# The second FFN product as Strassen's seven half-size products over pairs of 128-token tiles

## The chip, the cores and the metric

The kernel runs on one core of a Trainium2 chip. Its time is the device time of one execution in microseconds (us). The kernel before was timed three times.

## What is computed

```python
# attention: q, k, v are [4 batches, 8 heads, 768, 64], sort_net [4, 8, 8, 8]
P = sort_net                                   # five rounds: exp, row and column normalisation
k_sorted = einsum('bhij,bhjcd->bhicd', P, k_blocks)      # blocks of 96 rows
v_sorted = einsum('bhij,bhjcd->bhicd', P, v_blocks)
attn = softmax(q_b @ k_sorted_b.T / 8)         # within each of the 8 blocks
x = (attn @ v_sorted_b)  ->  [3072 tokens, 512]
# feed-forward network (FFN): w_in [512, 2048], w_out [2048, 512]
h = maximum(x @ w_in, 0)
out = (h * h) @ w_out                          # float32 [3072, 512]
```

Matrix products take bf16 operands and accumulate in fp32 in PSUM.

## The kernel before

The text counts the batches from 1 to 4 (the code's `b` from 0 to 3). A batch has 768 tokens. Attention of a batch ends in `xT`, the FFN's input, stored transposed: 128 features to a partition, four chunks of features (`kc`), all 3072 tokens along the free side. Both weights stay in SBUF as bf16 (`w_in_bf`, `w_out_bf`).

The FFN works on eight token groups of 384 (`ffn_unit(g)`, two to a batch). For a group it does

- the first product (L1009, tile `hp`): for each of 16 blocks of 128 hidden features (`nt`) four matmuls of 384 columns, each with a weight load of a 128x128 piece of `w_in_bf`. ScalarE takes the sum out of PSUM with a Relu (L1017), VectorE squares it (L1020) into `h2`.
- the second product (L1039, tile `op`): for each of three tiles of 128 tokens 16 matmuls of 512 columns, with pieces of `h2` as the loaded weights and rows of `w_out_bf` streaming. The 512 output columns of 128 tokens fill one PSUM bank. `put` copies them to SBUF (`ob`), and SyncE (SP) starts the DMA to `out`.
- the very last tile of 128 tokens is cut into 384 and 128 columns (`last_tile`, L1067), so that the last copy is small.

Three PSUM banks (pool `psf`, ring `rf`) serve both products; two double banks (`p2`) and one single bank (`p1`) serve attention.

The order of all instructions is fixed when the program is written. `Plan` keeps a list of operations with engine, assumed cost and dependencies. Attention's operations on TensorE (PE) have a due time in chunks of FFN work (table `DUES`: by batch and stage, K, V, N: sorting and loads of k and v; Z: turns of k and q by DMA; S: scores; A: attention times v; X: the turn of the result into `xT`). `Plan.run` plays the operations through and emits each engine's instructions in the resulting order. PE gets attention of batch n+1 between the FFN matmuls of batch n. For batches 2 to 4, X is a DMA transpose that SP issues (L920), only the last one of batch 2 goes through PE (L938); for batch 1 some go through PE and, in the second half, three through the DMA.

Loads of q, k and v for batches 3 and 4 are held back (L1157) until the attention of the batch before is in `xT`.

Of the kernel before, what the change touches and what calls it, by code (L numbers as in the profile page):

```python
# [8 lines left out]
FP32 = mybir.dt.float32  # L9
# [24 lines left out]
    (1, "X"): (40.0, 23.5, 37.0, 53.5),
    (2, "L"): (40.0,),
    (2, "N"): (75.5, 79.0),
    (2, "V"): (60.5, 82.5),
    (2, "Z"): (81.0, 82.5, 94.0, 83.5),
    (2, "S"): (86.0, 86.5, 96.0, 93.5),
    (2, "A"): (86.0, 88.0, 99.0, 94.5),  # L40
    (2, "X"): (97.5, 103.0, 103.0, 102.0),
    (3, "L"): (109.0,),
    (3, "N"): (111.5, 130.0),
    (3, "V"): (112.5, 144.0),
    (3, "Z"): (128.5, 139.0, 153.0, 149.0),
    (3, "S"): (144.0, 153.0, 158.0, 153.5),
    (3, "A"): (145.0, 153.5, 159.5, 154.5),
    (3, "X"): (150.5, 170.0, 236.5, 211.5),
}


# [55 lines left out]

class Plan:
# [6 lines left out]
    SWITCH = 0.1  # L115
    SLACK = {"DMA": 2.5, "WAY": 0.6}
# [19 lines left out]
    def run(self):  # L136
# [4 lines left out]
        while att or ffn or rest:  # L141
# [43 lines left out]
def kernel(  # L185
# [34 lines left out]
    psf = ctx.enter_context(tc.tile_pool(name="psf", bufs=3, space=bass.MemoryType.PSUM))  # L220
# [263 lines left out]
    def p_spread(e, i0):  # L484
        t = tiles["pt_ps", i0] = psf.tile([128, NQ, NH], FP32, tag="pf", name="pt_ps")
# [74 lines left out]
    def s_q(b, hp, p0, p1, due=0, after=None, eng=AD):  # L560
# [4 lines left out]
        def mm(e):  # L565
            qb = qkv[b][0]
            if b == 0:
                t["p"] = psf.tile([128, NA, n], BF16, tag="pf", name="qtp")
# [38 lines left out]
    def s_sort(u, t, due=0, early=False, eng=AD, own=False):  # L607
# [3 lines left out]
        def mm(e):  # L611
            src = qkv[u.b][t]
            if early:
                tp = ((ps1 if own else psf)
                      .tile([128, 512], FP32, tag="p1" if own else "pf", name="tp"))
# [115 lines left out]
    def s_vt(u, due=0, eng=AD, own=True):  # L731
# [95 lines left out]
    def s_turn(u):  # L827
# [10 lines left out]
        def k_blocks(e):  # L838
            nc.vector.tensor_copy(out=u.ksT[:, 0:S].rearrange("p (n x) -> p n x", n=NB),  # L839
                                  in_=kx_r[kx].rearrange("p (x n) -> p n x", n=NB))  # L840
# [4 lines left out]
        u.k_op = plan.add("DVE", 0.87, k_blocks, [k_op] + u.old)  # L845
# [69 lines left out]
    def s_xt(u, due=0, eng=AD, own=True):  # L915
        early = u.b == 0 and u.halves == (1,) and u.hp < HP - 1
# [17 lines left out]
        def mm(e):  # L934
            st["p"] = xtp = ((ps1 if own else psf)
                             .tile([128, u.ni, BLK], BF16, tag="p1" if own else "pf", name="xtp"))
# [21 lines left out]
    def f_piece(n):  # L958
# [3 lines left out]
        def mm(e):  # L962
            if kc == 0:
                tiles["hp", nt] = psf.tile([128, 512], FP32, tag="pf", name="hp")
            nc.tensor.matmul(  # L965
                out=tiles["hp", nt][:, 0:HS], lhsT=w_in_bf[:, kc, 128 * nt:128 * (nt + 1)],
                rhs=xT[:, kc, 0:HS], start=(kc == 0), stop=False)

        old = begun.setdefault((0, nt), [])
        if kc == 0:  # L970
            f_slot[nt], old = rf.take(pin=True)
        pe = plan.add("PE", 0.163, mm, [x_done[0, kc, 0], landed["w_in", 0]] + old)
        rf.use(f_slot[nt], pe)
        begun[0, nt].append(pe)

    def put(key, t, n, dst, pe, g):

        st = {}
        so, old = rob.take()

        def cp(e):
            st["ob"] = ffn.tile([128, d_model], FP32, tag="ob", name="ob", bufs=4)
            copy(e, st["ob"][:, 0:n], t[key][:, 0:n])

        op = plan.add(AD, cost_f(n), cp, [pe] + old)
        last = g == n_tok // HS - 2
        for p in ((slice(0, 32), slice(32, 64), slice(64, 128)) if last else (slice(0, 128),)):
            sp = plan.add("SP", 0.55, lambda e, p=p: nc.sync.dma_start(out=dst[p, :], in_=st["ob"][p, 0:n]), [op])
        rob.use(so, plan.add("WAY", 1.5, lambda e: None, [sp], tail=0.6))
        return op  # L990

    def ffn_unit(g):
        t0 = HS * g
        b, hf = g // 2, g % 2
# [223 lines left out]
```

## Time and profile before

| | |
|---|---|
| device time, three runs | 217.03, 217.30, 217.31 us; median 217.3 us |
| span of the profiled execution, first to last instruction | 215.4 us |
| own time of the profiled execution | the page gives only its span; the median is 1.9 us above it |
| busy: PE, PE weight loads, VectorE (DVE), ScalarE (ACT), GpSimd (POOL) | 210.0, 115.3, 110.3, 122.1, 28.2 us |
| mean granted TensorE clock | 1.000 |
| DMA | 31.92 MB, mean 148 GB/s |

How to read the rows that follow: a group row has line, engine, operation, output and inputs, count, then busy time in us, the mean ns of one, and the idle time before them with what ended it. A matmul's own duration contains the depth of the pipeline; how fast matmuls follow each other is read from the chain, whose pieces have start, length, engine, tile, line and count. In the waits each row is: engine and tile, waiting for what, us in total, times, longest.

### The profile page before, as it was taken

How to read it: one execution, taken by the hardware profiler on the slowest of the kernel's cores; microseconds unless marked ns; L12 is line 12 of the kernel's file. 1: busy time of each engine (PE TensorE's matmuls, PEld its weight loads, DVE VectorE, ACT ScalarE, POOL GpSimd, SP SyncE). 2: the span in 40 equal slices, each digit the busy share in tenths (PEclk: the TensorE clock that was granted, in tenths of full speed). 3: DMA queues.
4: the chain of work that ended last, by engine and by line, in shares of the span. 5: the costliest groups of instructions: out<-in, count | busy, mean ns of one | idle time of the engine just before them, and what ended most of it. 6: DMA issues, size and time to landing. Idle time of an engine off the chain costs nothing.

```text
span 215.4 us, 5104 instructions
## 1 busy us (share of the span) xinstructions
PE 210.0 (98%) x2035; PEld 115.3 (54%) x2035; DVE 110.3 (51%) x316; ACT 122.1 (57%) x251; POOL 28.2 (13%) x54
## 2 busy tenths in 40 slices
PE   7999999999999999999999999999999999999994
PEld 2466675446654555445655465445655465456543
DVE  6877676146795446335875047407775154015300
ACT  5786984238765278347774178318874376137421
POOL 7769221000000700000000420000000000000000
PEclk9999999999999999999999999999999999999999
DMA  6999999999987599199993699497988310221012
GB/s 154 204 202 207 206 207 211 185 186 259 243 173 108 80 233 215 29 189 223 171 226 96 111 191 216 89 214 160 155 228 110 101 49 3 49 67 30 0 52 97
DMA packets 47960, 31.92 MB, mean 148 GB/s; under 512 B 27392, under 2 KB 43008, under 8 KB 47936
## 3 DMA queue, kind: packets, MB, share of 16 engines
q1 hardware_dynamic: 35712, 18.35, 41.0%
q0 software_dynamic: 12224, 13.24, 37.7%
q8 instruction: 16, 0.26, 0.5%
q14 instruction: 8, 0.07, 0.1%
HBM read 29.70 MB, written 8.72 MB: 178 GB/s over the span
## 4 chain that ended last, share of the span: by engine, by line
PE 91%; DMA 4%; POOL 3%; ACT 1%; issue 1%; POOLq 0%
PE hp L1009 39%; PE op L1039 38%; DMA kb<-in_k_dram 4%; PE p L885 4%; PE p L694 3%; PE p L779 2%; PE op L1067 2%; POOL vb L330 1%; POOL kb L330 1%; PE p L659 1%; PE vbp L743 1%; POOL qb L330 1%; PE hp L965 0%; PE qtp L573 0%; PE xtp L938 0%
## 5 line engine op out<-in xcount | busy, mean ns | idle before, releaser
L1009 PE MATMUL hp<-xT,w_in_bf 128*128 128x384 bf16 x506 | 87.6, 326 | 0.0
L1039 PE MATMUL op<-w_out_bf,h 128*128 128x512 bf16 x368 | 85.1, 379 | 0.0
L1020 DVE TENSOR_TENSOR h<-h 128x384 bf16<-128x384 bf16 x128 | 44.0, 355 | 56.2 <-ACT h L1017 55.7
L1017 ACT ACTIVATE h<-hp 128x384 bf16<-128x384 f32 x128 | 61.7, 495 | 17.8 <-PE hp L1009 15.2
L1009 PEld LDWEIGHTS <-w_in_bf 128*128 128x128 bf16 x506 | 47.6, 98 | 32.4 <-issue 1.1
L1039 PEld LDWEIGHTS <-h 128*128 128x128 bf16 x368 | 33.9, 98 | 38.1 <-issue 1.4
L248 ACT COPY ob<-op 128x512 f32<-128x512 f32 (+2 forms) x25 | 14.2, 568 | 49.3 <-PE op L1039 46.8
L723 ACT ACTIVATE et<-p 96x384 bf16<-96x384 f32 x48 | 19.9, 488 | 6.1 <-PE p L694 6.1
L896 DVE TENSOR_TENSOR ao<-p,rec 96x512 bf16<-96x512 f32 x32 | 22.0, 687 | 1.3 <-DVE rec L895 0.2
L885 PEld LDWEIGHTS <-et 96*128 96x128 bf16 x256 | 11.3, 97 | 5.2 <-issue 0.7
L895 DVE RECIPROCAL rec<-p 96x8 f32<-96x8 f32 x32 | 6.4, 202 | 10.2 <-PE p L885 9.8
L1157 POOL COPY held<-xT 1x3 bf16<-1x3 bf16 (+1 forms) x2 | 0.4, 182 | 83.8 <-DMA xT<-ao 83.8
L250 DVE CAST vn<-p 128x768 bf16<-128x768 f32 x6 | 5.7, 957 | 7.5 <-PE p L779 7.4
L250 DVE CAST kn<-p 128x768 bf16<-128x768 f32 x5 | 4.8, 958 | 9.1 <-PE p L779 9.1
L885 PE MATMUL p<-vblk,et 96*128 96x65 bf16 x192 | 9.4, 193 | 0.0
L450 PE MATMUL p<-ones 128*128 128x512 bf16 (+1 forms) x27 | 8.2, 441 | 1.1 <-DVE ones L274 1.1
L694 PEld LDWEIGHTS <-kvT 64*128 64x128 bf16 x256 | 6.2, 94 | 5.3 <-issue 3.4
L839 DVE COPY kvT<-kx 128x768 bf16<-128x768 bf16 x10 | 8.5, 850 | 0.0
L248 ACT CAST vn<-p 128x768 bf16<-128x768 f32 x6 | 4.8, 797 | 5.8 <-PE p L779 5.8
L330 POOL DMA_DIRECT2D kb<-in_k_dram x10 | 6.5, 649 | 4.5 <-DMA w_in_bf<-in_moe_w_in_dram 2.0
L248 ACT CAST kn<-p 128x768 bf16<-128x768 f32 x5 | 4.0, 806 | 4.7 <-PE p L779 4.7
L330 POOL DMA_DIRECT2D vb<-in_v_dram x10 | 6.3, 635 | 2.1 <-DMA w_in_bf<-in_moe_w_in_dram 1.1
(81 smaller groups left out, 119.0 us busy)
## 6 DMA issues: line engine op xcount, KB each, us to landing
out_dram<-ob SPq DMA_DIRECT2D x20, 256.0 KB, 3.1
v_way<-vn SPq DMA_DIRECT2D x6, 396.0 KB, 6.0
vblk<-v_way SPq DMA_DIRECT2D x6, 396.0 KB, 4.2
vb<-in_v_dram POOLq DMA_DIRECT2D x6, 384.0 KB, 11.8
kb<-in_k_dram POOLq DMA_DIRECT2D x6, 384.0 KB, 10.5
qb<-in_q_dram POOLq DMA_DIRECT2D x6, 384.0 KB, 13.3
w_in_bf<-in_moe_w_in_dram POOLq DMA_DIRECT2D x4, 512.0 KB, 10.0
w_out_bf<-in_moe_w_out_dram POOLq DMA_DIRECT2D x4, 512.0 KB, 14.7
```

The source lines that it names most:

```text
L248: nc.scalar.copy(out=out, in_=in_)
L250: nc.vector.tensor_copy(out=out, in_=in_)
L330: nc.gpsimd.dma_start(out=dst, in_=src)
L694: nc.tensor.matmul(out=scp[:, h, BLK * n:BLK * (n + 1)], lhsT=u.ksT[64 * h:64 * (h + 1), HS * hf + BLK * n:HS * hf + BLK * n + 128], rhs=( ...
L723: nc.scalar.activation(out=et[:, h, 0:HS].rearrange("p (n c a) -> p n c a", c=C0, a=NA), in_=st["p"][0:96, h, 0:HS].rearrange("p (n a c) - ...
L839: nc.vector.tensor_copy(out=u.ksT[:, 0:S].rearrange("p (n x) -> p n x", n=NB), in_=kx_r[kx].rearrange("p (x n) -> p n x", n=NB))
L885: nc.tensor.matmul(out=oup[:, h, 66 * n:66 * n + D + 1], lhsT=et_r[u.et[hf]][:, h, BLK * n:BLK * n + 128], rhs=(u.vs[:, NQ * hf + n, h, 0: ...
L896: nc.vector.tensor_tensor(out=u.ao[:, n0:n0 + NQ, :, :].rearrange("p n e d -> p e n d"), in0=ov[:, :, :, 0:D], in1=rec[:, :, :, None].to_b ...
L1009: nc.tensor.matmul(out=t["hp", nt][:, 0:HS], lhsT=w_in_bf[:, kc, 128 * nt:128 * (nt + 1)], rhs=xT[:, kc, t0:t0 + HS], start=(kc == 0), sto ...
L1017: nc.scalar.activation(out=t["h1", nt], in_=t["hp", nt][:, 0:HS], func=AF.Relu)
L1020: nc.vector.tensor_tensor(out=t["h2"][:, nt, :], in0=t["h1", nt], in1=t["h1", nt], op=ALU.mult)
L1039: nc.tensor.matmul(out=t["op", mt], lhsT=t["h2"][:, nt, 128 * mt:128 * (mt + 1)], rhs=w_out_bf[:, nt, :], start=(nt == 0), stop=(nt == NT ...
```

## The change

Batch 1 keeps its two groups of 384 tokens and its plain second product (`plain_block`). Batches 2 to 4 are cut into nine groups of 256 tokens. Each group is a pair of 128-token tiles. Write the squared hidden values of a pair as a 2x2 block matrix (rows: the two tiles; columns: hidden features 0-1023 and 1024-2047), and `w_out` likewise (features by output columns 0-255 and 256-511). The plain product takes eight block products, Strassen's scheme (in Winograd's form) takes seven and some sums.

- First product: per group 16 x 4 matmuls of 256 columns, two blocks `nt` into one bank; Relu and square work on 512 columns at once; the square may go to ScalarE or VectorE.
- Weight sums: eight VectorE subtractions of 128x1024 elements make four 1024x256 sums of `w_out` (`w_sum`), once, after both halves of `w_out` have landed.
- Sums of hidden values (`make_sums`, L1201): per pair six VectorE instructions, four over 512 elements and two over 1024 a partition, into columns of `xT` that are free by then.
- Seven products (`product`, L1241) of eight matmuls of 256 columns. Two or three of them accumulate in one PSUM bank, so that the partial sums gather there: p1, p6, p7 and p4 in bank "a"; p2 in "b"; p5 and p3 in "c". Between them three copies of 256 columns go to SBUF (`keep`: after p1, p5 and p6) and three VectorE additions read PSUM and such a copy and write the output tile (`join`: after p2, p3 and p7). A last copy takes what p4 completes. A product that accumulates over what was just copied waits for that copy or addition.
- `LEAD` and `LAG` set how many blocks of the next group's first product stand ahead of a pair's products, and how many between p7 and p4.
- The table `DUES` has other numbers, `cost`s of some operations allow ScalarE or VectorE, the rings for `kx`, `qi` and `ob` have 2, 3 and 3 buffers (before 3, 4 and 4), the three FFN banks are taken least recently used first, and in the second half of batch 1 one X goes through the DMA instead of three, two more through PE.

```diff
@@ table DUES, one row of many
-    (3, "X"): (150.5, 170.0, 236.5, 211.5),
+    (3, "X"): (171.5, 136.03125, 138.5, 161.5),
+TURNED = 1
+LEAD = (0, 0, 2, 8, 0, 2, 12, 0, 12, 14, 1)
+LAG = (0, 0, 2, 1, 2, 1, 2, 0, 2, 2, 0)
@@ s_xt
-        early = u.b == 0 and u.halves == (1,) and u.hp < HP - 1
+        early = u.b == 0 and u.halves == (1,) and u.hp < TURNED
@@ new: the sums of w_out
+            for name, dst, a, b in (("T1", t1, b_part(1, js), b_part(0, js)),
+                                    ("T2", t2, b_part(3, js), t1),
+                                    ("T3", t3, b_part(3, js), b_part(1, js)),
+                                    ("T4", t4, b_part(2, js), t2)):
+                op = plan.add("DVE", 0.69, ... nc.vector.tensor_tensor(
+                    out=dst, in0=a, in1=b, op=ALU.subtract), [op, *lands], due=WSUM)
@@ ffn_unit(g), second product
-        for mt in range(HS // 128 - (g == n_tok // HS - 1)):
-            for part in range(4):
-                    for nt in range(4 * part, 4 * part + 4):
-                        nc.tensor.matmul(
-                            out=t["op", mt],
-                            lhsT=t["h2"][:, nt, 128 * mt:128 * (mt + 1)],
-                            rhs=w_out_bf[:, nt, :], ...)
@@ new: pair_block, the sums of hidden values (h0, h1: first tile; h2, h3: second tile)
+            for js in halves:
+                one(0, js, h_view(2, js), h_view(3, js), ALU.add, ...)
+            for js in halves:
+                one(1, js, s_view(0, js), h_view(0, js), ALU.subtract, ...)
+            o4 = one(3, whole, h_view(1, whole), s_view(1, whole), ALU.subtract, ...)
+            o3 = one(2, whole, h_view(0, whole), h_view(2, whole), ALU.subtract, ...)
@@ new: the seven products
+        A = {1: ("h", 0), 2: ("h", 1), 3: ("s", 3), 4: ("h", 3), 5: ("s", 0), 6: ("s", 1), 7: ("s", 2)}
+        W = {1: ("b", 0), 2: ("b", 2), 3: ("b", 3), 4: ("t", 2, "T4"), 5: ("t", 3, "T1"),
+             6: ("t", 0, "T2"), 7: ("t", 1, "T3")}
+        def p1a(): make_sums(); product(1, early, "a", True)
+        def p2a(): product(2, range(0, late2.start), "b", True)
+        def p1b(): keep("s1", "a", product(1, range(NJ - 1, NJ), "a", False))
+        def p2b(): c11(product(2, late2, "b", False))
+        def p5():  keep("s5", "c", product(5, range(NJ), "c", True))
+        def p6():  keep("s2", "a", product(6, range(NJ), "a", False, [cbuf["s1"][1]]))
+        def p3():  st["c12"] = join("s2", "c", product(3, range(NJ), "c", False, [cbuf["s5"][1]]), ...)
+        def p7():  st["c22"] = join("s5", "a", product(7, range(NJ), "a", False, [cbuf["s2"][1]]), ...)
+        def p4():  op = fin(left, product(4, range(NJ), "a", False, [st["c22"]]))
+        return ([p1a, p2a, p1b, p5, p6, p3, p7, p2c, p4] if last else
+                [p1a, p2a, p1b, p2b, p5, p6, p3, p7, p4])
```

How the order of instructions changes at three places (rows that only repeat are left out; `[waits ...]` names what an instruction waits for: DMAHW a DMA queue, Activation ScalarE).

PE, the end of batch 3, where the last attention of batch 4 stands and its first FFN matmul follows. `vblk` and `et` are attention's operands, `h_2475` the squared hidden values, the four DMAHW waits are the four turns of X into `xT`. Before:

```order
L885 MATMUL p_1_79<-vblk_118,et_139 128x65 [waits Activation_49]
...
L1039 MATMUL op<-w_out_bf,h_2475 128x512
...
L1009 MATMUL hp<-xT,w_in_bf 128x384 [waits DMAHW1_49]
L1009 LDWEIGHTS w_in_bf
L1009 MATMUL hp<-xT,w_in_bf 128x384 [waits DMAHW5_49]
```

After, `wsum_160` belongs to p6, `w_out_bf,xT` to p3, `wsum_161` to p7, `wsum_162` to p4:

```order
L921 MATMUL p_1_79<-vblk_121,et_140 128x65 [waits Activation_49]
...
L1241 MATMUL pf_82<-wsum_160,xT 128x256 [waits Activation_49]
...
L1241 MATMUL pf_80<-w_out_bf,xT 128x256 [waits Activation_49]
...
L1241 MATMUL pf_82<-wsum_161,xT 128x256 [waits Activation_49]
...
L1241 MATMUL pf_82<-wsum_162,hid 128x256 [waits DVE_49]
...
L1066 MATMUL pf_81<-xT,w_in_bf 128x256 [waits DMAHW4_49]
```

Between the last attention matmul and the first that needs batch 4's `xT` stood 20 matmuls of 512 columns; now stand four products, 32 matmuls of 256 columns, with four waits for ScalarE or VectorE.

VectorE, the last pairs of the program (`hid`: squares, `xT<-`: sums of hidden values, `ob`: joins). Before, nothing but squares:

```order
L1020 TENSOR_TENSOR h_3065<-h_3177 128x384
L1020 TENSOR_TENSOR h_3065<-h_3185 128x384
L1020 TENSOR_TENSOR h_3065<-h_3193 128x384
L1020 TENSOR_TENSOR h_3065<-h_3201 128x384
L1213 UNCONDITIONAL_BRANCH
```

After:

```order
L1083 TENSOR_TENSOR hid<-h_3454 128x2x256
L1201 TENSOR_TENSOR xT<-hid 128x2x256
L1201 TENSOR_TENSOR xT<-hid 128x4x256
L1201 TENSOR_TENSOR xT<-xT,hid 128x2x256
L1201 TENSOR_TENSOR xT<-hid,xT 128x4x256
L1272 TENSOR_TENSOR ob<-pf_82,xT 128x256
L1272 TENSOR_TENSOR ob<-pf_81,xT 128x256
L1272 TENSOR_TENSOR ob<-pf_80,xT 128x256
```

Behind the last square stand four sums and then the three joins of the last pair; p5, p6, p3 and p7 on PE read those sums.

PE, the end of the program, before:

```order
L1039 MATMUL op<-w_out_bf,h_3065 128x512
L1067 LDWEIGHTS h_3065
L1067 MATMUL op<-w_out_bf,h_3065 128x384 [waits Activation_49]
...
L1067 MATMUL op<-w_out_bf,h_3065 128x128 [waits Activation_49]
```

After (p3, p7, the second half of p2, p4):

```order
L1241 MATMUL pf_82<-w_out_bf,xT 128x256 [waits Activation_49]
...
L1241 MATMUL pf_81<-wsum_161,xT 128x256 [waits Activation_49]
...
L1241 MATMUL pf_80<-w_out_bf,hid 128x256
...
L1241 MATMUL pf_81<-wsum_162,hid 128x256 [waits DVE_49]
```

The last product waits for VectorE's join of p7, with four matmuls of 256 columns between the two, and the last copy and the last DMA have 256 columns instead of 128.

More of the change, by code (lines that the diff above doesn't have):

```diff
@@ L105, in idle, with __init__, take, touch @@
                 return slot
+class Lru(Ring):
+    def __init__(self, n):
+        super().__init__(n)
+        self.order = list(range(n))
+    def take(self, pin=False):
+        slot = next(s for s in self.order if s not in self.pinned)
+        if pin:
+            self.pinned.add(slot)
+        old, self.users[slot] = self.users[slot], []
+        slot = Slot(slot)
+        self.holders[slot] = slot
+        self.touch(slot)
+        return slot, old
+    def touch(self, slot):
+        self.order.remove(slot)
+        self.order.append(int(slot))
 class Plan:
@@ L115 @@
     SWITCH = 0.1
+    UNIT = 0.742
     SLACK = {"DMA": 2.5, "WAY": 0.6}
@@ L567, in mm @@
             if b == 0:
-                t["p"] = psf.tile([128, NA, n], BF16, tag="pf", name="qtp")
+                t["p"] = in_bf16(s1, NA, n)
             else:
@@ L978, in put, with store, out_tile @@
+    def store(ob, so, row, deps, cols=slice(0, d_model), parts=(slice(0, 128),)):
+        for p in parts:
+            sp = plan.add("SP", 0.55, lambda e, p=p: nc.sync.dma_start(
+                out=out[row + p.start:row + p.stop, cols], in_=ob()[p, cols]), deps)
+        rob.use(so, *deps, plan.add("WAY", 1.5, lambda e: None, [sp], tail=0.6))
+    def out_tile():
         st = {}
         so, old = rob.take()
-        def cp(e):
-            st["ob"] = ffn.tile([128, d_model], FP32, tag="ob", name="ob", bufs=4)
-            copy(e, st["ob"][:, 0:n], t[key][:, 0:n])
@@ L1056, in last_tile, with get @@
[L1056 to L1076 removed]
+        def get():
+            if "ob" not in st:
+                st["ob"] = ffn.tile([128, d_model], FP32, tag="ob", name="ob", bufs=3)
+            return st["ob"]
@@ new lines, in out_tile, with plain_block, part, down @@
+        return get, so, old
+    def plain_block(row, c):
+        st = {}
+        items = []
+        def part(p):
+            if p == 0:
+                st["s"], st["old"] = rf.take()
+            def down(e):
+                for nt in range(4 * p, 4 * p + 4):
+                    nc.tensor.matmul(out=pf_r[st["s"]], lhsT=hid[:, nt, TT * c:TT * (c + 1)],
+                                     rhs=w_out_bf[:, nt, :], start=(nt == 0), stop=(nt == NT - 1))
+            pe = plan.add("PE", 0.865, down, [squares[c, nt] for nt in range(4 * p, 4 * p + 4)]
+                          + [landed["w_out", p]] + (st["old"] if p == 0 else []), ffn=True)
+            rf.touch(st["s"])
+            h_users[c] = [pe]
+            rf.use(st["s"], pe)
+            if p == 3:
+                ob, so, old = out_tile()
+                op = plan.add(AD, cost_f(512), lambda e: copy(e, ob(), pf_r[st["s"]]), [pe] + old)
+                rf.use(st["s"], op)
+                store(ob, so, row, [op])
+        items.extend(lambda p=p: part(p) for p in range(4))
+        return items
@@ L1173 @@
     for due, _, stage, b in sorted(todo, key=lambda x: x[:2]):
-        stage(int(due))
-    for g in range(n_tok // HS):
-        ffn_unit(g)
+        stage(due)
+    ffn_all()
     started = filled = False
```

427 lines of the change are left out of this document (298 added, 129 removed).

## The prediction, made before the changed kernel ran

> **What bounds the kernel now.** I read the page first (busy time, chain that ended last), then the waits of PE, then the chain in order of time, then groups and timeline for prices.
>
> ```profile
> PE 210.0 (98%) x2035; PEld 115.3 (54%) x2035; DVE 110.3 (51%) x316; ACT 122.1 (57%) x251; POOL 28.2 (13%) x54
> PE 91%; DMA 4%; POOL 3%; ACT 1%; issue 1%; POOLq 0%
> PE hp L1009 39%; PE op L1039 38%; DMA kb<-in_k_dram 4%; PE p L885 4%; PE p L694 3%; PE p L779 2%; PE op L1067 2%; POOL vb L330 1%; POOL kb L330 1%; PE p L659 1%; PE vbp L743 1%; POOL qb L330 1%; PE hp L965 0%; PE qtp L573 0%; PE xtp L938 0%
> ```
>
> The waits of PE (in total, times, longest), first and last of its five rows:
>
> ```profile
> PE p L450 <- DVE ones L274: 1.1, 1, 1.1
> ...
> PE tp L623 <- DMA kb<-in_k_dram: 0.2, 1, 0.2
> ```
>
> So PE carries 91% of the chain and waits for almost nothing; the two FFN products alone are 77%. Whatever shortens PE's stream shortens the kernel, as long as the stream stays without gaps. VectorE and ScalarE are half idle, but their answers now have to come in time.
>
> **How fast matmuls follow each other.** The chain in order of time (start, length, piece):
>
> ```profile
> 19.53 0.17 PE xtp L938 x4
> ...
> 166.43 0.25 PE p L885 x8
> 166.68 4.32 PE op L1039 x20
> 170.99 10.40 PE hp L1009 x64
> 181.39 10.36 PE op L1039 x48
> ...
> 209.06 3.51 PE op L1067 x32
> 212.57 0.02 issue
> 212.59 0.27 ACT ob L248
> ```
>
> 10.40/64 = 162.5 ns for 384 columns, 10.36/48 = 215.8 ns for 512: 53.3 ns for 128 columns, so 109.2 ns for 256 by the same line. The last piece has 16 matmuls of 384 and 16 of 128 columns: 3.51 - 16 x 0.1625 = 0.91, or 57 ns for 128 columns, again on the line. Each of these matmuls has its own 128x128 weight load, which takes longer than that:
>
> ```profile
> L1067 PEld LDWEIGHTS <-h 128*128 128x128 bf16 x32 | 2.5, 98 | 1.3
> ```
>
> 98 ns of load did not hold up a stream of 57 ns, so it will not hold up one of 109. I take 0.1092 us for a 256-column matmul; the bounds from the nearest rows are 0.057 and 0.1625.
>
> The Trainium skill speaks against halving the columns ("TensorE: Matmul & The Clock Gate", section "Back-to-back issue gap"): for streams of load-and-matmul pairs it gives about 81 ns at 128 columns and 131 ns at 512. By a line through these (an estimate from that page) 256 columns would cost 98 ns, 504 of them 49.2 us against 37.7 us for 288 of 512, and the first product would lose 12.4 us too: some 24 us slower. The trace disagrees at both ends (57 and 216 ns), so the sum does not use it.
>
> **PE's work.**
> - Second product of batches 2 to 4: 18 tiles x 16 = 288 matmuls before, of which 272 of 512 columns (58.70 us) and the last tile (3.51 us): 62.2. After: 9 pairs x 7 x 8 = 504 of 256 columns: 55.0. -7.2 us.
> - First product of these batches: 6 x 64 = 384 matmuls x 0.1625 = 62.4 before, 9 x 64 = 576 x 0.1092 = 62.9 after. +0.5 us.
> - Batch 1's second half: two more X through PE, four transposes of 0.17 us each. +0.3 us. The two DMA transposes that go lay beside other work.
>
> Sum: -6.4 us, if PE never waits.
>
> **VectorE and ScalarE.** The prices, by group and shape:
>
> ```profile
> L1017 ACT ACTIVATE h<-hp 128x384 bf16<-128x384 f32 x128 | 61.7, 495 | 17.8 <-PE hp L1009 15.2 <-DVE h L1020 1.1
> L1020 DVE TENSOR_TENSOR h<-h 128x384 bf16<-128x384 bf16 x128 | 44.0, 355 | 56.2 <-ACT h L1017 55.7
> L896 DVE TENSOR_TENSOR ao<-p,rec 96x512 bf16<-96x512 f32 x32 | 22.0, 687 | 1.3 <-DVE rec L895 0.2
> L248 ACT COPY ob<-op 128x512 f32<-128x512 f32 x23 | 13.5, 585 | 46.8 <-PE op L1039 46.8
> L499 DVE TENSOR_TENSOR w_all<-mask,pt 128x256 bf16<-128x256 bf16 x2 | 0.8, 420 | 0.0
> L248 ACT COPY ob<-op 128x384 f32<-128x384 f32 x1 | 0.5, 479 | 2.0 <-PE op L1067 2.0
> L248 ACT COPY ob<-op 128x128 f32<-128x128 f32 x1 | 0.3, 266 | 0.4 <-PE op L1067 0.4
> L375 DVE TENSOR_TENSOR fold<-ident 128x64 bf16<-128x64 bf16 x1 | 0.2, 173 | 0.0
> ```
>
> - Sums of bf16 in SBUF: 64 elements 173 ns, 384 elements 355 ns, so 0.57 ns each: 0.43 us for 512 and 0.72 for 1024. The slow bound goes by the 256-element row (420 ns, 1.3 ns for each element beyond 64): 0.75 and 1.4 us. I take the fast values, since the squares' row has the same types and plain layout. Per pair 4 x 0.43 + 2 x 0.72 = 3.2 us, in all 28 us; the eight weight sums 5.8 us.
> - Joins: 27 x 0.42 = 11 us (0.687 for 512 elements is the upper bound, 0.3 by half of it the lower). Copies to SBUF of 256 columns on ScalarE: halfway between 266 and 479, 0.37 us each, 10 us.
> - Squares: 128 x 0.355 = 45.4 us before; after, VectorE has 59 of 512 and 23 of 384 elements, 33.5, and ScalarE the other 22. Five kvT copies move to ScalarE as well.
>
> That leaves VectorE near 140 us and ScalarE near 136 us of about 212: no bound as a total. The weight sums stand among batch 1's squares, where VectorE has room, but they wait for the landing of `w_out`:
>
> ```profile
> 16.00:32.00 16.00, 15.47 (x297) 11.17 (x298) 11.70 (x29) 13.07 (x25) 7.80 (x16) 1.00 1.24 207
> 32.00:47.20 15.20, 15.16 (x115) 7.14 (x112) 7.11 (x17) 5.53 (x10) 0.87 (x2) 1.00 1.24 190
> 37.88 0.04 issue
> ```
>
> (Stretch, its length, then busy PE, PEld, DVE, ACT, POOL, the granted clock 1.00; then from the chain the gap of PE ahead of the last quarter of the first tile's product, which needs the last piece of `w_out`.) VectorE goes from 7.1 to some 13 of 15.2 us there. Behind a weight sum that waits stand two squares of the first group, not due at PE before 37.9 either: I take 0, with 1 us as the upper bound (two of 0.36 late behind 0.72), and nothing below it.
>
> The table's new order of batch 1's attention moves the same matmuls about in these two stretches. PE's idle 0.5 us there is all that it can win; a loss of the same size is my other end; I take 0. Three instead of four `ob` buffers: a pair fills two in 13 us, and a store lands in 3.1 us, so nothing waits, unless SP holds the store behind a turn. The same room covers the shorter rings of `kx` and `qi`, whose turns stand on SP in the same order (0; up to 1 us).
>
> ```profile
> out_dram<-ob SPq DMA_DIRECT2D x20, 256.0 KB, 3.1
> ```
>
> **Hand-offs inside a pair.** This is the new wait. The bank that a product accumulates into must first be read by `keep` or `join`.
>
> ```profile
> 170.83 5.36 PE L1009 MATMUL hp<-xT,w_in_bf 128*128 128x384 bf16 x32
> 172.39 0.49 ACT L1017 ACTIVATE h<-hp 128x384 bf16<-128x384 f32 x1 [0.16 <-PE hp L1009]
> 172.91 0.36 DVE L1020 TENSOR_TENSOR h<-h 128x384 bf16<-128x384 bf16 x1 [0.29 <-ACT h L1017]
> 18.52 0.56 ACT qz L248
> 19.07 0.04 issue
> 19.11 0.41 PE p L885 x8
> ```
>
> The second block's stream ends at 170.83 + 8 x 0.1625 = 172.13, ScalarE starts at 172.39: 0.26 us. Back from ScalarE to PE: 0.04. So a hand-off takes 0.26 + 0.37 + 0.04 = 0.67 us by copy, 0.72 by join. The cover is the product between: eight matmuls, 0.87 us (0.98 for p6). It holds by 0.15 to 0.3 us, unless another ScalarE or VectorE instruction (0.36 to 0.69) stands ahead. Between products of the last two full pairs (groups 8 and 9) nothing of attention stands: 0. The five pairs before them with attention around (2 to 6) I give 0.2 us each, 1.0 in all (0 to 0.6 each). The sums of hidden values come in time: with no block of lead, the last square ends 0.26 + 0.60 + 0.03 + 0.43 = 1.3 us behind the last first-product matmul, the four sums behind it end at 3.6, and p3, which needs the last, stands at 16 + 16 matmuls, 3.5 us.
>
> In the last pair only four matmuls (0.44 us) cover p7's join of 0.72: +0.3.
>
> **The start of batch 4.** The waits and X's DMA:
>
> ```profile
> 166.26 0.41 PE L885 MATMUL p<-vblk,et 96*128 96x65 bf16 x8
> 166.78 0.20 DVE L895 RECIPROCAL rec<-p 96x8 f32<-96x8 f32 x1
> 167.02 0.69 DVE L896 TENSOR_TENSOR ao<-p,rec 96x512 bf16<-96x512 f32 x1
> DMA to landing us min/median/max: 2.8/3.6/12.0
> ```
>
> The last attention stream of batch 4 ends at 166.68, its normalisation at 167.71, its turn lands 2.8 to 3.6 us later: 3.8 to 4.6 behind the stream; PE came to it after 4.32 us (20 matmuls). Now 32 matmuls stand there, 3.5 us, and a sum of 0.72 us stands on VectorE ahead of that normalisation, of which about 0.3 delays it. So X is 4.1 to 4.9 behind, PE is there at 3.5: a wait of 0.6 to 1.4 us, and p4 without cover (0.72) lies within it. I take 1.0; the lower bound is 0 (a landing at 2.8 and p4's own wait already counted), the upper 2.1 (p4's 0.7 on top).
>
> **The tail.** Copy of 256 instead of 128 columns: +0.1. Its DMA:
>
> ```profile
> out_dram<-ob SPq DMA_DIRECT2D x7, 64.0 KB, 1.6
> out_dram<-ob SPq DMA_DIRECT2D x3, 128.0 KB, 2.2
> ```
>
> 128 KB instead of 64: at most +0.6; I take 0.4, since the last one lands alone.
>
> **Sum.** -6.4 (PE) + 1.0 (hand-offs) + 0.3 (last pair) + 1.0 (batch 4) + 0.5 (tail) = -3.6 us. The profiled span 215.4 becomes 211.8; the median of the runs lies 1.9 above the span, so 217.3 - 3.6 = 213.7 us. A run can tell about 0.2% (0.4 us) from no change. With all waits at 0 the sum is 211.4; with five pairs at 0.6, weight sums at 1 and batch 4 at 2.1, 217.3 - 6.4 + 3.0 + 1.0 + 2.1 + 0.3 + 0.7 = 218.0, all mishaps at once.
>
> **The rivals.**
> 1. Hand-offs decide (slower). If ScalarE's exponentials and Relus stand ahead of the copies, each of the four hand-offs of a pair loses up to 0.6 - 0.2 = 0.4 us, 1.6 a pair. Against it: attention brings PE matmuls too, which are cover, and three pairs have none. From 3.6/9 = 0.4 us a pair beyond my sum it is no gain; with 0.9 in the six pairs of batches 2 and 3, 213.7 - 1.0 + 5.4 = 218.1 us. 7%.
> 2. A floor under a load-and-matmul pair, as the skill's rule has it. At 1080 pairs 3.3 ns each eat the gain. The straight line through 128, 384 and 512 columns leaves no such room; if only a tenth of the 98 ns load came out, 213.7 + 10.6 = 224 us. 2%.
> 3. Batches 3 and 4 are not ready earlier. FFN shortens by some 2.1 us a batch, but the loads are let go only when the attention before is done; if loads and attention take as long as before, PE waits 2.1 us at two boundaries: 213.7 - 1.0 + 4.2 = 216.9. For it: at batch 4 the margin is gone already. Against it: nearly all attention waits for its due place on PE, not the reverse. 10%.
> 4. No wait anywhere, and the covers hold: 211.4 us or a little below. 9%.
> 5. The gain is lost in small waits to within 0.2%: 3%.
>
> The forecast has the remaining 69%. Faster: 69 + 9 and most of rival 3 (10): 88%; same 3%; slower 7 + 2 = 9%. The range 211.0 to 216.2 takes in the forecast and rival 4, and leaves out 7 + 2 + 3, some half of rival 3 and a little below.
>
> **What will show it.** The chain's pieces of 64 first-product matmuls at 6.99 us, eight of a product at 0.87. The waits of PE for ScalarE and VectorE at L1241 sum to 1 to 2 us; the wait for X's DMA at the first L1066 of batch 4 is about 1. VectorE near 140 us busy, its sums 0.43 and 0.72. The clock 1.0. The prediction is wrong if the 256-column matmul is not 109 ns, or if PE's waits exceed 6 us.

## The result, and the profile after

| | before | after |
|---|---|---|
| device time, median of the runs beside each other | 217.17 us (216.97 to 217.31) | 215.53 us (215.26 to 215.86) |
| ratio, 95% interval | | 0.9927 [0.9913, 0.9941] |
| profiled execution: device time, span | span 215.4 us | 215.62 us, span 213.8 us |

The kernel became 1.6 us faster, and the interval leaves no room for "no change"; the forecast was 3.6 us. 215.5 us lies inside the stated range.

The page of the kernel after: busy times, then the chain that ended last, by engine.

```profile
PE 205.9 (96%) x2435; PEld 154.7 (72%) x2435; DVE 136.6 (64%) x355; ACT 138.6 (65%) x272; POOL 28.2 (13%) x54
...
PE 80%; ACT 10%; DVE 5%; issue 3%; DMA 1%; DVEq 0%; ACTq 0%
```

PE lost 4.1 us of busy time, and its share of the chain fell from 91% to 80%: 15% of the span now hangs on ScalarE or VectorE. A share of the chain is not idle time of PE; its gaps, below, are far smaller. The waits of PE (total, times, longest), the three largest rows that are new:

```profile
PE p L730 <- ACT kvT L284: 0.9, 2, 0.4
PE pf L1241 <- DVE xT L1201: 0.6, 1, 0.6
PE pf L1241 <- DVE ob L1272: 0.5, 1, 0.5
```

The chain in order of time (start, length, piece). The first line begins batch 2, the second is the first full run of 64 first-product matmuls near the start of batch 3; then the end of batch 3, batch 4, and the last pair.

```profile
76.11 7.86 PE pf L1066 x72
...
125.11 6.99 PE pf L1066 x64
132.10 5.24 PE pf L1241 x48
...
166.80 0.25 PE p L921 x8
167.05 2.64 PE pf L1241 x24
169.69 0.02 issue
169.71 0.43 DVE ob L1272
170.15 0.04 issue
170.19 1.03 PE pf L1241 x8
171.22 12.23 PE pf L1066 x112
...
209.25 0.44 DVE ob L1272
209.73 1.05 PE pf L1241 x8
...
210.80 0.37 ACT ob L284
```

6.99/64 and 5.24/48 are 109.2 ns, the price of the forecast to the digit. Batch 4, from 171.22 to the last copy at 210.80, takes 39.6 us; before it took 41.6 (170.99 to 212.59). So where nothing of attention stands between the pairs, the two microseconds a batch arrive. They do not in batches 2 and 3, as the stretches of one batch each show, first of before, then of after (stretch, its length, busy PE, PEld, DVE, ACT, POOL, then the granted clock, DMA share and GB/s):

```profile
75.40:123.40 48.00, 48.00 (x418) 25.34 (x416) 25.34 (x60) 27.78 (x58) 2.00 (x5) 1.00 0.87 166
123.40:171.00 47.60, 47.60 (x419) 25.35 (x417) 24.94 (x60) 27.22 (x58) 1.80 (x3) 1.00 0.88 167
```

```profile
76.10:124.20 48.10, 46.82 (x555) 38.68 (x553) 32.70 (x71) 34.00 (x64) 3.81 (x7) 1.00 0.83 161
124.20:171.20 47.00, 46.05 (x555) 38.68 (x553) 33.83 (x75) 31.35 (x60) 0.00 (x0) 1.00 0.83 167
```

Batch 2 is no shorter and batch 3 by 0.6 us. PE stood idle for 1.3 and 0.95 us there (stretch less busy time), before not at all.

Busy time counts the tail of a matmul as work, so I also took gaps from the records: start of a matmul minus start of the one before, less its stream time by the line of the prediction (53.3 ns for 128 columns plus 2.5). From 50 us on, gaps over 0.15 us sum to 0 before and 4.4 us after. These are the ones of after:

| at | gap | what PE waited for |
|---|---|---|
| 61.46, 64.55 | 0.25, 0.38 | second half of batch 1: a Relu, then exponentials, on ScalarE behind a kvT copy |
| 87.8, 88.9 | 0.18, 0.27 | first pair of batch 2: a sum of hidden values, then a cast of k on ScalarE behind a late copy to SBUF |
| 98.89 | 0.58 | kvT copied by ScalarE, first of batch 3's attention |
| 110.72 | 0.21 | exponentials behind a kvT copy on ScalarE |
| 119.74, 121.45 | 0.23, 0.80 | third pair of batch 2: a copy to SBUF behind sums of hidden values, then a sum behind such a copy |
| 149.27 | 0.60 | kvT copied by ScalarE, first of batch 4's attention |
| 170.19 | 0.68 | p4's uncovered join at the start of batch 4 |
| 209.73 | 0.24 | p7's join in the last pair |

The kvT copy is the copy of the sorted k (`kx`) into the order that the scores read. Before, VectorE made all ten of them (two in batch 2, four each in batches 3 and 4); now ScalarE makes five. The row of before, then the two of after by engine:

```profile
L839 DVE COPY kvT<-kx 128x768 bf16<-128x768 bf16 x10 | 8.5, 850 | 0.0
...
L284 ACT COPY kvT<-kx 128x768 bf16<-128x768 bf16 x5 | 8.0, 1591 | 0.0
L286 DVE COPY kvT<-kx 128x768 bf16<-128x768 bf16 x5 | 4.2, 850 | 0.0
```

The list of operations assumes 0.80 us for the one and 0.87 for the other. The timeline of after at the first of these gaps: the copy ends at 98.83, and the scores, which PE was ready for, start at 98.89. The Relu (L1074) queued behind it is late too, and VectorE's square behind that.

```profile
97.25 1.58 ACT L284 COPY kvT<-kx 128x768 bf16<-128x768 bf16 x1
98.73 1.09 ACT L1074 ACTIVATE h<-pf 128x512 bf16<-128x512 f32 x2
98.89 0.51 PE L730 MATMUL p<-qz,kvT 64*128 64x96 bf16 x16 [0.42 <-ACT kvT L284]
99.36 0.43 DVE L1083 TENSOR_TENSOR hid<-h 128x512 bf16<-128x512 bf16 x1 [1.28 <-ACT h L1074]
```

The timeline around the 0.80 us gap:

```profile
118.20 1.03 DVE L1201 TENSOR_TENSOR xT<-hid 128x512 bf16<-128x512 bf16 x2
119.31 0.76 ACT L284 COPY xT<-pf 128x256 f32<-128x256 f32 x2 [1.61 <-DVE xT L1201]
119.72 0.43 DVE L1201 TENSOR_TENSOR xT<-xT,hid 128x512 bf16<-128x512 bf16 x1 [0.49 <-ACT xT L284]
120.24 0.43 DVE L1272 TENSOR_TENSOR ob<-pf,xT 128x256 f32<-128x256 f32 x1
120.70 0.69 DVE L1201 TENSOR_TENSOR xT<-hid,xT 128x1024 bf16<-128x1024 bf16 x1
121.45 1.05 PE L1241 MATMUL pf<-w_out_bf,xT 128*128 128x256 bf16 x8 [0.63 <-DVE xT L1201]
```

ScalarE's copy to SBUF (`keep`) waits 1.61 us for VectorE's *sums*, and a sum then waits for the copy, though they share no data: both write to the tile `xT`, in different places.

### The profile page after: what moved, and what is told of

Read it like the earlier page. It is cut to its first block, busy times and chain, and to the rows that moved or that the text cites. A ratio compares the mean times of both kernels' runs of the same rounds, so it can differ in the third digit from the quotient of the medians.

```text
span 213.8 us, 5958 instructions
## 1 busy us (share of the span) xinstructions
PE 205.9 (96%) x2435; PEld 154.7 (72%) x2435; DVE 136.6 (64%) x355; ACT 138.6 (65%) x272; POOL 28.2 (13%) x54
## 4 chain that ended last, share of the span: by engine, by line
PE 80%; ACT 10%; DVE 5%; issue 3%; DMA 1%; DVEq 0%; ACTq 0%
PE pf L1066 33%; PE pf L1241 23%; PE pf L1153 9%; PE p L730 3%; PE p L921 3%; ACT h L1074 2%; ACT kvT L284 2%; PE p L815 2%; ACT et L759 2%; ACT hid L1081 1%; DVE xT L1201 1%; PE p L695 1%; DMA p_sb<-in_sort_net_dram 1%; PE p L486 1%; PE vbp L779 1%
## 5 line engine op out<-in xcount | busy, mean ns | idle before, releaser
L1066 PE MATMUL pf<-xT,w_in_bf 128*128 128x256 bf16 (+1 forms) x698 | 89.4, 282 | 0.1
L1066 PEld LDWEIGHTS <-w_in_bf 128*128 128x128 bf16 x698 | 66.1, 98 | 14.6 <-issue 1.4
L1074 ACT ACTIVATE h<-pf 128x512 bf16<-128x512 f32 (+1 forms) x104 | 56.9, 568 | 20.5 <-PE pf L1066 19.4
L1083 DVE TENSOR_TENSOR hid<-h 128x512 bf16<-128x512 bf16 (+1 forms) x82 | 33.1, 405 | 30.4 <-ACT h L1074 29.2
L1241 PEld LDWEIGHTS <-xT 128*128 128x128 bf16 x288 | 27.4, 98 | 5.0 <-DVE xT L1201 1.2
L1241 PE MATMUL pf<-wsum,xT 128*128 128x256 bf16 x216 | 27.1, 273 | 0.1
L1241 PEld LDWEIGHTS <-hid 128*128 128x128 bf16 x216 | 20.6, 98 | 3.5 <-issue 1.1
L1153 PE MATMUL pf<-w_out_bf,hid 128*128 128x512 bf16 x96 | 22.6, 379 | 0.0
L1241 PE MATMUL pf<-w_out_bf,hid 128*128 128x256 bf16 x144 | 18.0, 273 | 0.0
L1153 PEld LDWEIGHTS <-hid 128*128 128x128 bf16 x96 | 8.7, 97 | 9.2 <-issue 0.2
L1201 DVE TENSOR_TENSOR xT<-hid 128x512 bf16<-128x512 bf16 (+1 forms) x27 | 13.0, 510 | 0.6
L1241 PE MATMUL pf<-w_out_bf,xT 128*128 128x256 bf16 x72 | 9.4, 273 | 0.6 <-DVE xT L1201 0.6
L1241 PE MATMUL pf<-wsum,hid 128*128 128x256 bf16 x72 | 9.3, 272 | 0.6 <-DVE ob L1272 0.5
```

What stands on the lines that cost most here:

```text
L1066: nc.tensor.matmul(out=pf_r[st["s"]][:, n * m:n * (m + 1)], lhsT=w_in_bf[:, kc, 128 * nt:128 * (nt + 1)], rhs=xT[:, kc, t0:t0 + n], start= ...
L1074: nc.scalar.activation(out=st["h1"][:, 0:n * len(nts)], in_=pf_r[st["s"]][:, 0:n * len(nts)], func=AF.Relu)
L1083: nc.vector.tensor_tensor(out=dst, in0=h1, in1=h1, op=ALU.mult)
L1153: nc.tensor.matmul(out=pf_r[st["s"]], lhsT=hid[:, nt, TT * c:TT * (c + 1)], rhs=w_out_bf[:, nt, :], start=(nt == 0), stop=(nt == NT - 1))
L1201: lambda e: nc.vector.tensor_tensor(out=s_view(n, js), in0=a, in1=bb, op=op), deps + st["old", n])
L1241: nc.tensor.matmul(out=pf_r[st[bank]][:, cols], lhsT=a, rhs=r, start=(first and j == 0), stop=(j == NJ - 1), skip_group_check=n in (3, 4, ...
```

## The experiments

Two theories stood at the start. A: the price of the kvT copy on ScalarE. B: a false dependency between the copies (`keep`) and the sums, since both lie in `xT`. All experiments ran beside the kernel before; times are medians.

**The `keep` copies in a tile of their own** (B alone; "keeps apart" below):

```diff
-            k %= 4
+            k %= 3
-            buf = xT[:, k, rb + 2 * TT:rb + 6 * TT].bitcast(FP32)
+            buf = w_all.rearrange("p a b c -> p (a b c)")[:, 512 * k:512 * (k + 1)].bitcast(FP32)
```

> The copies of partial sums (keep) go to the tile w_all, which batch 1 and 2's sorting is done with, instead of to free columns of xT. Same order on every engine. Theory A (the wait comes from the kvT copies on ScalarE, 1.58 us each instead of the 0.80 that the program assumes): the gap of PE ahead of p3 in the third pair of batch 2 (0.80 us, with 0.23 ahead of p6) stays, and the time stays within 0.3 us of the changed kernel's 215.5. Theory B (ScalarE's copies and VectorE's sums wait for each other only because both lie in xT, where the program sees them overlap): both gaps shrink to under 0.3 us together, the copies' wait for VectorE's sums (ACT xT L284 <- DVE xT L1201, 4.6 us in 4) is gone, and the kernel gains 0.7 to 1.0 us: 214.6.

Measured 214.83 us, ratio 0.9891 [0.9863, 0.9920]. The order of all instructions stayed; only waits went. Of the program's rows for the first pair of batch 2, a `keep` and a 1024-element sum, after and then here:

```
L284 COPY xT<-pf_80 128x256 [waits DVE_49,PE_49]
L1201 TENSOR_TENSOR xT<-hid,xT 128x4x256 [waits DVE_49,Activation_49]

L284 COPY w_all<-pf_80 128x256 [waits PE_49]
L1201 TENSOR_TENSOR xT<-hid,xT 128x4x256 [waits DVE_49]
```

On the timeline the copy now starts ahead of the sum, and p3 nearly in time:

```profile
118.28 0.37 ACT L284 COPY w_all<-pf 128x256 f32<-128x256 f32 x1 [1.02 <-PE pf L1241]
118.70 0.42 DVE L1201 TENSOR_TENSOR xT<-xT,hid 128x512 bf16<-128x512 bf16 x1
119.37 0.68 DVE L1201 TENSOR_TENSOR xT<-hid,xT 128x1024 bf16<-128x1024 bf16 x1
120.10 1.05 PE L1241 MATMUL pf<-w_out_bf,xT 128*128 128x256 bf16 x8
```

The gaps of 0.18, 0.27, 0.23 and 0.80 us became 0.17 in all, 1.3 us less, and the profiled span fell by 1.3 (213.8 to 212.5), but this execution, of 214.23 us, lies 0.6 below the run's median. The medians differ by 0.7 us, and the two intervals just overlap. So the traces show the wait and that it is false; of its price the runs say 0.7 to 1.3 us. Why the program sees an overlap (probably because it compares address ranges, and a range over four feature chunks spans the copies between them) was not tried.

**The five kvT copies on VectorE, in the same order** (A alone), then **both edits**:

```diff
-            copy(e, u.ksT[:, 0:S].rearrange("p (n x) -> p n x", n=NB),
+            copy("DVE", u.ksT[:, 0:S].rearrange("p (n x) -> p n x", n=NB),
```

> The five kvT copies that stood on ScalarE are issued on VectorE at the same place of the order (0.85 us each there instead of 1.58). Nothing else moves. Theory A: PE's waits for them (0.58 and 0.60 us ahead of attention's scores in batches 2 and 3) go, and ScalarE, which ran without a pause from 108 to 118 us, is 0.8 us earlier in the third pair of batch 2, so that gap (0.80 + 0.23) goes as well: 2.0 us in all, 213.5. Theory B: only the two waits for the copies go, 1.2 us, 214.3, and the gap of 0.80 stays within 0.3 of its size.

> Both edits together. Theory A: as with the kvT copies alone, 213.5. Theory B: the two gains add, 1.2 + 0.9, 213.4. What then remains of PE's waits in batches 2 to 4: the uncovered join at the start of batch 4 (0.68 us), the last pair (0.24) and the evictions of the first pair (0.5).

Measured 215.74 us, ratio 0.9935 [0.9909, 0.9960], and with both 215.17 us, 0.9908 [0.9876, 0.9940]: the first can't be told from after, and the second gained nothing over the separate tile. In the first trace both kvT gaps were gone, but others came behind the other three copies: 0.77 us at 61.1, 0.54 at 111.8 and 0.59 at 164.2. After had 0.25 and 0.38 at 61 and 64, 0.21 at 110.7 and none at 164. The second trace has gaps at the same places (0.77, 0.34, 0.59 us) and one of its own: at 114.9 us PE waits 1.3 us for the transfer of the sorted v.

```profile
PE p L921 <- DMA vblk<-v_way: 1.3, 1, 1.3
```

That execution took 216.41 us, 1.2 above the run's median, so it does not stand for the run. I took the two times for the fall of A; the later runs showed that only this remedy fell.

**Plain second product in the new groups of 256 tokens:**

```diff
-            pairs.append([pair_block(t0, t0 + TT, c, c + 1, t0 // S, t0 + 2 * TT == n_tok)])
+            pairs.append([plain_block(t0, c) + plain_block(t0 + TT, c + 1)])
-                if g > 1:
+                if False:
```

> The pairs of batches 2 to 4 compute the second product plainly again (two tiles of 16 matmuls of 512 columns each); groups of 256 tokens, table of due times, buffers and the weight sums (unused) stay. If the seven products save what their matmuls say, PE's stream grows by 9 x (32 x 0.2158 - 56 x 0.1092) = 7.1 us; the hand-offs of the pairs (about 2.2 us of gaps) go. So 215.5 + 7.1 - 2.2 = 220.4 us (219.5 to 222.5). This is slower than the kernel before by what the rest of the change costs, about 3 us. The rival: the gain of the matmuls was already smaller, and this comes out below 219.

(The second edit leaves out the move of p4 by `LAG`; the weight sums are still made.) Measured 221.73 us, ratio 1.0233 [1.0183, 1.0284]. So against the same grouping the seven products gain 6.2 us, of the 7.1 that the count of matmuls promises; the rest of the change, in an order made for the seven products, costs 4.7 us over before (221.73 against 217.02 beside it). How much of that is the order was not separated.

**More cover for p4 at the start of batch 4** (keeps apart):

```diff
-LAG = (0, 0, 2, 1, 2, 1, 2, 0, 2, 2, 0)
+LAG = (0, 0, 2, 1, 2, 1, 2, 2, 2, 2, 0)
```

> The keeps have a tile of their own, and the fourth product of a pair is now followed by two later stretches of work before its join is needed (its LAG entry 0 becomes 2). Theory C (the 0.68 us at the start of batch 4 is the uncovered join of that product and nothing else): the gap goes, 214.1 to 214.4 against 214.83 with the keeps apart alone. Rival (what the prediction had: X itself is late by about 1 us there, and the join only hides it): the gap moves behind the next matmuls of batch 4, 214.7 to 215.1.

Measured 215.14 us, ratio 0.9907 [0.9890, 0.9924]; span 213.2 against 212.5. Theory C fell and the prediction's mechanism held: the chain now waits for X.

```profile
165.63 0.25 PE p L921 x8
165.88 1.19 PE pf L1241 x11
167.06 2.82 DMA xT<-ao
169.89 0.04 issue
169.93 0.71 PE pf L1066 x5
170.64 0.87 PE pf L1241 x8
```

X can be used 4.05 us after the last attention stream (165.88 to 169.93; the forecast said 4.1 to 4.9). In the kernel after, the chain has PE there at 167.05 + 4.17, so at most about 0.1 us is to be had from better cover of the join: 2.64 us of products and 0.87 of p4 make 3.5, X needs 4.05, and the join's 0.68 us lie nearly all beside that wait. The records of after agree: the last turn of X, issued at 168.24 us, lands at 171.07, and the first matmul that needs X starts at 171.06.

**The order made again with the true price** (keeps apart):

```diff
-        u.k_op = plan.add(AD, (0.8, 0.87), k_blocks, [k_op] + u.old)
+        u.k_op = plan.add(AD, (1.59, 0.87), k_blocks, [k_op] + u.old)
```

> The keeps have a tile of their own, and the program's own price for the kvT copy on ScalarE is 1.59 us in place of 0.8 us, so that the order of work is made again with it. Theory A2 (the two gaps of 0.58 and 0.60 us cost because the order was made with a wrong price; moving the copy in a fixed order only shifted them): 213.6 to 214.2. Rival (VectorE and ScalarE together have no room around the attention's start, whoever copies; the wait turns up elsewhere): 214.6 to 215.2.

Measured 216.37 us, ratio 0.9965 [0.9938, 0.9991]: slower than the keeps apart alone. All ten copies went to VectorE and no wait for kvT is left, but attention of batch 4 came later. The waits of PE:

```profile
PE pf L1241 <- DVE ob L1272: 0.9, 1, 0.9
PE pf L1066 <- DMA xT<-ao: 0.9, 1, 0.9
```

The due times were found for the old prices; made again by the same table, the order loses in another place.

**The copies on GpSimd** (keeps apart; all ten kvT copies by `nc.gpsimd.tensor_copy`, at a price of 1.6 us in a new order):

> The keeps have a tile of their own, and the five kvT copies of batches 1 to 4 that ScalarE or VectorE shared go to GpSimd with all the others of that line, priced at 1.6 us in the order. Theory A2/B2 (VectorE and ScalarE have no room there and GpSimd, busy 13%, has): both gaps go, 213.6 to 214.2. Rival (GpSimd's copy takes longer than 1.6 us and the attention waits for it in every unit): 215 to 219, with PE waiting for POOL at L730.

Measured 220.02 us, ratio 1.0119 [1.0096, 1.0142], above both forecasts. One takes 1.62 us there, so it probably lengthens each unit's way from k to X (the new order was not separated from that), and PE pays at X of batch 4 rather than at the scores:

```profile
L875 POOL COPY kvT<-kx 128x768 bf16<-128x768 bf16 x10 | 16.2, 1624 | 82.2 <-DMA kx<-kn 77.9 <-PE p L730 2.5 <-PE pf L1241 1.8
```

```profile
PE pf L1066 <- DMA xT<-ao: 3.4, 2, 2.9
```

The wait is not the whole price. Behind it the granted clock stood at half, and 24 matmuls started in 5 us in place of 48 (stretch, its length, busy PE with its matmuls, PEld, DVE, ACT, POOL, then the granted clock, DMA share and GB/s):

```profile
174.00:179.00 5.00, 4.97 (x24) 3.45 (x24) 0.85 (x2) 1.43 (x3) 0.00 (x0) 0.50 0.00 0
182.00:187.00 5.00, 5.00 (x48) 4.50 (x46) 3.84 (x9) 4.11 (x8) 0.00 (x0) 1.00 0.00 0
```

The first 109 first-product matmuls of batch 4 took 14.57 us in this execution, at 109.2 ns they would take 11.9: 2.7 us more by the clock, beside a wait of 2.9.

**Three X of batch 1 by DMA, as before the change** (`TURNED = 3`, keeps apart):

> The keeps have a tile of their own, and three of batch 1's four X turns go by DMA as before the change (TURNED 1 becomes 3), so that 16 matmuls by PE are gone. The prediction's term (two X more through PE cost 0.3 us, and with the evictions nearer 0.5): 214.3 to 214.6. Rival (X by DMA comes late in batch 1, which is why it was changed; or the new order meets other waits): 214.8 to 215.6.

Measured 216.98 us, ratio 1.0000 [0.9988, 1.0012], above both forecasts. (The two X are eight transposes on PE, not 16: the weight loads fall from 2435 to 2427.) The new order meets two other waits: 1.1 us for the normalisation ahead of the one X that is left to PE, and 1.0 us for a Relu that stands behind a kvT copy of 1.60 us and three exponentials on ScalarE. The 0.3 us of the two X can't be seen apart from that; the run tells nothing of their price.

**The same copy, reading adjacent elements** (keeps apart; the order of work unchanged):

```diff
+            if e == "ACT":
+                copy(e, u.ksT[:, 0:S], kx_r[kx])
+            else:
...
```

> The keeps have a tile of their own; the order of work is kept, and ScalarE's five kvT copies read the source in its own order (adjacent elements) in place of every eighth element; the k rows of those units then stand in another order, so this leaves out a part of the computation. If the distance between the elements that ScalarE reads makes its copy 1.59 us, it falls to about 0.8 us. Theory A3 (the two gaps of 0.58 and 0.60 us ahead of the scores are the copy's missing price and cost in full): both gaps go and nothing else moves, 213.5 to 213.9. Rival (what comes behind, X of batch 4 above all, is the limit, and the time comes back as a wait for X): 214.4 to 215.0.

Measured 213.13 us, ratio 0.9826 [0.9797, 0.9855]: 1.7 us faster than the keeps apart, the intervals apart as well, and 0.4 below A3's own range. This decides for A3.

```profile
L284 ACT COPY kvT<-kx 128x768 bf16<-128x768 bf16 x5 | 4.2, 838 | 0.0
```

Nothing of the program but the length of five instructions changed, from 1.59 to 0.84 us, about what the list of operations assumes. The gaps at 98 and 148 us are gone, and so are those in the second half of batch 1 (0.25 and 0.38 us around 61 and 64), where a kvT copy on ScalarE stands too. One gap is new: 0.48 us at 113.66, where PE now waits for exponentials and the transfer of the sorted v. From 50 us on, gaps over 0.15 us sum to 1.6 us, against 3.1 with the keeps apart (two more there, 0.23 and 0.32 us, are places where matmul records are missing) and 4.4 after. The spans of the two traces, 212.9 and 212.5 us, do not show this, because this execution began the second half of batch 1 1.7 us later (48.87 against 47.20 us). From that matmul to the end it takes 164.0 us, with the keeps apart 165.3. So the price of the five copies is 1.2 us by these traces and 1.7 by the medians.

**Adjacent reading, distant writing** (keeps apart):

```diff
+                copy(e, u.ksT[:, 0:S].rearrange("p (n x) -> p x n", n=NB),
+                     kx_r[kx].rearrange("p (x n) -> p x n", n=NB))
```

> The keeps have a tile of their own; the same copy with the full result, but ScalarE walks the source in its own order and writes every 96th element. If reading with a distance is what is slow: 0.8 us a copy, and the time of the kernel as with the adjacent copy (213.5 to 213.9 by theory A3, 214.4 to 215.0 by the rival). If a distance on either side costs the same: 1.59 us again and 214.6 to 215.0.

Neither: 232.27 us, ratio 1.0699 [1.0658, 1.0739]. Writing with 192 bytes between elements costs ScalarE far more than reading with 16 (side and distance changed together, so the run does not say which of them costs):

```profile
L284 ACT COPY kvT<-kx 128x768 bf16<-128x768 bf16 x5 | 20.1, 4024 | 0.0
```

2.4 us more in each of five copies than with the keeps apart gave 17 us more (214.83). The scores, the Relus and the exponentials behind them on ScalarE come late: PE's five longest gaps behind 50 us, 2.59, 3.01, 2.56, 3.01 and 1.99 us, sum to 13.2. Around the end of each of the first four the granted clock fell to 0.50 for about 3.4 us, and its mean over the execution was 0.970. By an estimate from these numbers, half of 13 to 14 us, that cost some 6.5 us more.

**Two versions with the full result.** Only the two copies that PE waited for go to VectorE; then, besides, the other three are halved between the engines:

```diff
+            copy("DVE" if (b, hp) in ((2, 0), (3, 1)) else e,
...
+            if e == "ACT" and (b, hp) not in ((2, 0), (3, 1)):
+                copy("ACT", out[:, 0:4], in_[:, 0:4])
+                copy("DVE", out[:, 4:8], in_[:, 4:8])
```

> The keeps have a tile of their own, the order of work is kept, and of ScalarE's five kvT copies only the two that PE waited for (the first of batch 3 and the first of batch 4 to be copied there) go to VectorE, where one takes 0.85 us; the full result. Theory A3: the gaps of 0.58 and 0.60 us go and the other three copies, left on ScalarE, cause none of the gaps that came when all five went: 213.4 to 213.9. Rival (VectorE has no room at these two places either, and a gap of 0.3 to 0.6 us comes back behind each copy): 214.4 to 215.0.

> As the kernel with the two copies on VectorE, and each of the three copies left on ScalarE is halved: four of the eight blocks on ScalarE (about 0.8 us), four on VectorE (about 0.43 us). Theory A3 (with adjacent reading no gap was left in batch 1 and at these units, so 0.8 us on ScalarE is short enough): 213.0 to 213.5, the gaps of 0.25 and 0.38 us around 61 and 64 us gone too. Rival (the half on VectorE is what makes new gaps there, as when all five copies were moved): 213.8 to 214.8.

Measured 214.05 us, ratio 0.9850 [0.9824, 0.9875], and 214.01 us, ratio 0.9866 [0.9833, 0.9898]. Both gaps are gone in the first, as A3 said; in its place one of 0.65 us came at 113.5 us (exponentials on ScalarE), so the median fell by 0.8 us instead of 1.2, to between the two forecasts. Halving moved the median no further, as its rival said: the halves took 0.89 us on ScalarE and 0.49 on VectorE, and 0.43 us of gaps remain at 60.2 and 0.25 at 161.5, in an execution of 213.19 us, 0.8 below the run's median. The best kernel with the full result is thus 3.1 us faster than before, 1.5 us faster than the change as it was made; the two cannot be told apart.

## Why the prediction missed the size

The side was right, and so was the outline: PE's work fell as counted, and small waits took part of it back. But most of these waits were not the ones forecast, and the size was off by 2 us. Term by term, in us (measured: gaps and pieces of the profiled execution of after; PE's work is the count times the measured price, and the line on batch 1 is what the other lines leave of the sum):

| term | forecast | measured |
|---|---|---|
| PE's work, 109.2 ns a matmul | -6.4 | -6.4 |
| kvT copies on ScalarE | 0 | +1.4 |
| pairs, hand-offs | +1.0 | +1.5 |
| start of batch 4 | +1.0 | +0.7 |
| last pair | +0.3 | +0.2 |
| tail | +0.5 | +0.2 |
| batch 1, and gaps under 0.2 us | 0 | about +0.8 |
| sum | -3.6 | -1.6 |

- **The step that failed** is one sentence: "Five kvT copies move to ScalarE as well." It stands beside ScalarE's total and got no duration, no bound and no waiter, so that its term in the sum was 0 without a reason. The trace of before had the copy only on VectorE (10 x 850 ns), with no copy of that shape from SBUF on ScalarE; the 0.80 us of the list of operations is what a copy of adjacent elements takes (0.84). It took 1.59 us, stands straight ahead of the scores, and ScalarE's queue behind it feeds the Relus. In the trace of after its gaps are 0.58, 0.60 and 0.21 us; shortening the copies alone, batch 1's among them, gave back 1.7 us in the medians and 1.2 between the traces.
- **Hand-offs**: 1.0 us was put on the products' banks, and these were nearly without gaps, as the cover of 0.87 us foresaw. What came was a wait of another kind, between instructions that share a tile but no data; it accounts for 1.3 of the 1.5 us. That 1.0 and 1.5 lie near each other is chance. The prediction followed what each product needs, not the waits that the program writes. The rows of the program's order show it, with their waits.
- **Start of batch 4**: no wait for X shows in the chain of after, as forecast it would; p4's join does, 0.68 us. With p4 covered, the wait for X appeared (1.1 us). The mechanism was right: X came 4.0 us behind the last attention stream, just ahead of the 4.1 to 4.9 forecast. The size was 0.3 too large.
- **Tail**: the copy took 0.37 us as said; behind its end lie 2.6 us (211.17 to 213.8) as against 2.5 before (212.86 to 215.4). A 128 KB store that lands alone cost 0.1 us more than one of 64 KB, not 0.4.
- **Batch 1**: batch 2 starts 0.7 us later than before (76.11 against 75.43); 0.3 of it was counted within PE's work. The gaps of 0.25 and 0.38 us behind a kvT copy lie there, and they went with the shortened copies. Other runs that keep this order start batch 2 between 75.8 and 77.0 us (the distant writing apart), so the rest of that line is not settled.
- The prices of VectorE held: sums 0.42 and 0.69 us (0.43 and 0.72 said), joins 0.42, VectorE 136.6 us busy (140 said), ScalarE 138.6 (136 said).
- **Rivals**: the floor under a load-and-matmul pair is refuted at 256 columns, 109.2 ns with a load of 98 ns each; the Trainium skill's figures ("TensorE: Matmul & The Clock Gate", section "Back-to-back issue gap") would have put 98 ns there (an estimate by a line between its two figures), and the measurement decides. No hand-off made it slower, and PE waited for no late transfer in batches 3 and 4, though X at batch 4 had at most 0.1 us to spare. With both unforeseen waits taken away (keeps apart, adjacent reading) the kernel came to 213.13 us, 0.6 below the forecast; that version leaves the k rows of five units in another order.

## What to carry to other kernels

A change that moves an instruction to another engine has a price per instruction, shape and access pattern: where the trace has no row for it, bound it and name who waits, even for five instructions. Buffers borrowed from a tile that another engine is writing can bring waits without shared data, and the waits in the program's order show them. In an order fixed by a table, a gap was closed best here by shortening what it waits for, next best by moving the one instruction in it: moving all its like, or making the order again, opened gaps of the same size elsewhere.

## What the runs showed of the hardware

- ScalarE's copy of 128x768 bf16 in SBUF: 0.84 us from adjacent elements, 1.59 us from elements 16 bytes apart, 4.02 us to elements 192 bytes apart. VectorE copies with the same 16 bytes between the elements that it reads in 0.85 us; GpSimd takes 1.62. The Trainium skill ("Advanced Engine Details and Errata", section "SBUF Cachelines") says that SBUF has lines of 16 bytes and that an access that falls on another line each time pays a penalty. ScalarE's read agrees, 0.75 us more for 768 elements that each lie on a line of their own; the page gives no figure, and VectorE's 0.85 us cannot be set against it, since no run here has VectorE's copy of the shape from adjacent elements in the same order.
- Matmul streams of 256 columns with a 128x128 weight load each run at 109.2 ns, on the same line as 128, 384 and 512 columns. Of 1030 pairs of such matmuls that follow each other in the trace of after, 1004 start 108 to 112 ns apart.
- Long gaps of PE cost a second time, by the clock. With the copies on GpSimd (a gap of 3.08 us) and with distant writing (2.59, 3.01, 2.56 and 3.01 us) the granted clock fell to 0.50 at each, for 6.8 us in all in the first run and about 3.4 us each time in the second. At gaps of 1.99 us (distant writing), 1.42 (both edits) and 1.27 (p4 covered) it did not fall.
